# A mixed attention and spectral kernel: even row frequencies split once more, four of eight folds moved late, first loads in fixed order

## The chip, the cores and the metric

The kernel runs on one core of a Trainium2 chip. The metric is the device time of one execution in microseconds (us). Engines are named as the profile names them: PE is TensorE (PEld its weight loads), DVE is VectorE, ACT is ScalarE, POOL is GpSimd, SP is SyncE, which here only issues transfers.

## The reference, cut to what matters

```python
x = A_x                                   # (1, 2048, 640), fp32
g = sigmoid((x * gate_w).sum(-1, keepdims=True))
# a: attention with 32 heads of 20 over 8 positions s, s-2, ..., s-14
qkv = x @ wqkv
logits = einsum("bhsd,bhswd->bhsw", q, kg) * scale      # masked where s - 2w < 0
a = einsum("bhsw,bhswd->bhsd", softmax(logits), vg) reshaped @ wo
# b: a filter in the two-dimensional spectrum
X = rfft2(x) * (B_w_r + 1j * B_w_i)
b = irfft2(X, s=(2048, 640))
return g * a + (1 - g) * b
```

## The kernel before, in words

The 2048 positions are laid out as 128 partitions by 16 columns j (position 16p + j), called `NJ`. Even and odd j are treated apart, since attention steps by two.

**Projection** (`qkv`, line 703). Eight calls, one for each parity and each of four head groups. Each handles eight j; for one j fifteen multiplications (the operands split in a high and a low fp32r part, three products for each of five row chunks) sum 480 columns in one PSUM bank, taken in turn from `BP`, seven banks. ScalarE copies the bank to `ev`, and each second copy is stored to `qkv_d` in device memory.

**Attention** (`attend`, line 743). Sixteen units (parity, h) of four heads in the order `UNITS`. A unit loads keys, queries and values; for four pairs of rows jj it makes the products `pr` (on VectorE with the query in PSUM, or on GpSimd where `POOL_PR` says so), reduces them on VectorE to `L`, does the softmax, then makes `pv` on GpSimd and reduces it on VectorE to `o`, which goes to `o_d`. The last two units run pair by pair.

**Folds** (`fold`, line 824). The row transform of x over its 640 features uses symmetry: for each pair q of columns j, the row is folded into sums and differences of mirrored elements, twice, in place, in six instructions: 320 for odd frequencies, 320 for even ones, cosine and sine apart. Folds 0 to 5 are stored to `f_d` and reloaded by `load_f` (line 845); 6 and 7 stay. `cols` (line 849) then multiplies each by a table over partitions (twenty fp32 instructions `z` for one q) and ScalarE puts the result in `zg`, whose place is that of `xe`, the even inputs of the projection.

**Frequency groups** (`freq`, line 871). Sixteen groups g. `row` multiplies five chunks of `zc` by `bt`: three multiplications for `v`, three for `u`, of 321, 161 and 160 columns. Then column steps `xa` to `xd`, the filter `wp` (GpSimd and VectorE), and `g` back to `zg`. **Spatial** (`spatial`, line 996) goes back over features with `gt` (`oa`, `ob`) and over partitions (`ha`, `hb`); odd j keep theirs in `ho`, even j finish. **Even and odd projections** (`project_even`, `project_odd`, lines 1078 and 1094) load attention's result, transpose it (`oTp`), and multiply by `wo` (`woa`, `wob`, thirty multiplications for each j). Even ones are done as soon as the even units are; odd ones are last, and `ye` and `y` sum their spectral part on GpSimd.

**What sets the order.** Every operation is recorded by `Plan.record` first. `Plan.order` then gives each a cost (`Plan.cost`), runs a list scheduler backward and forward several times, disturbs the due times `AGAIN` times (`MOVE`, `SEED`) and keeps the best; `Plan.issue` emits the operations in that fixed order (line 639 is where they are issued, and so stands in all rows of the trace). Loads from inputs get an earliest time (`op.early`). Each engine's queue is in order; so is each issuing queue.

Of the kernel before, what the change touches and what calls it, by code (L numbers as in the profile page):

```python
# [31 lines left out]
def dft_tables():  # L32
# [7 lines left out]
    ke, ko = PERM[:161], PERM[161:]  # L40
    kb = PERM[2:161]
# [9 lines left out]
    def half(n, *ends):  # L51
# [3 lines left out]

    bt = np.zeros((640, 642))
    bt[0:161, 0:161] = np.cos(tau * np.outer(np.arange(161), ke) / D) * half(161, 0, 160)
    bt[161:321, 161:321] = np.cos(tau * np.outer(np.arange(160), ko) / D) * half(160, 0)
    bt[321:480, 323:482] = -np.sin(tau * np.outer(np.arange(1, 160), kb) / D)
    bt[480:640, 482:642] = -np.sin(tau * np.outer(np.arange(1, 161), ko) / D) * half(160, 159)  # L60
# [58 lines left out]
    d = np.arange(161)  # L119
# [5 lines left out]
    gt[0:161, 0:161] = np.cos(tau * np.outer(ke, d) / D) * ck(ke)  # L125
    gt[161:321, 161:322] = np.cos(tau * np.outer(ko, d) / D) * ck(ko) * (d < 160)
    gt[321:480, 322:483] = -np.sin(tau * np.outer(kb, d) / D) * ck(kb) * ((d > 0) & (d < 160))
    gt[480:640, 483:644] = -np.sin(tau * np.outer(ko, d) / D) * ck(ko) * (d > 0)
    gt = np.concatenate(
        [gt[0:128, 0:161], gt[128:256, 0:322], gt[256:384, 161:483], gt[384:512, 322:644], gt[512:640, 483:644]], 1  # L130
    )
    f = np.float32
    return {
        "t_fc": np.concatenate([fc, back[0].T, back[1].T], 1).astype(f),
# [7 lines left out]
class Op:  # L142
    __slots__ = ("i", "eng", "name", "call", "busy", "lat", "size", "preds", "succs", "chain", "tail", "start", "end", "early", "group", "of", "two")
# [12 lines left out]
class Plan:  # L156
# [65 lines left out]
    def record(self, eng, name, fn, a, k):  # L222
        op = Op()
        op.i, op.eng, op.name, op.chain, op.group = len(self.ops), eng, name, self.chain, self.group
        op.preds, op.succs, op.size, op.early, op.two = set(), [], 0, False, False
# [15 lines left out]
    def cost(self, op, out, ins, k):  # L241
        n = max(int(np.prod(v.shape[1:])) for v in [out] + ins[:1])
        if op.name == "dma_start":
            op.busy, op.lat = {"SP": 0.45, "ACT": 0.45, "POOL": 1.0}[op.eng], LAND
            op.size = int(np.prod(out.shape)) * 4
            op.early = not hasattr(ins[0].tensor, "tag")
        elif op.eng == "PE":
            n = int(np.prod(out.shape[1:]))
            if op.name == "transpose":
                op.busy = 0.109  # L250
            elif ins[-1].dtype == F32R:
                op.busy = n / 2400 + 0.018
            else:
                op.busy = 4 * n / 2400 + 0.006
# [23 lines left out]
    def order(self):  # L278
# [134 lines left out]
    def forward(self):  # L413
# [10 lines left out]
        while len(done) < len(ops):  # L424
# [47 lines left out]
TURNS, AGAIN, MOVE, SEED = 6, 100, 2.0, 2  # L472
# [7 lines left out]
FOLD = 14.0  # L480
# [25 lines left out]
class Mixer:  # L506
# [17 lines left out]
    def places(self, pp, dr, sb):  # L524
# [26 lines left out]
        self.er, self.xor = ring("e0", "e1"), ring("raw0", "raw1", "raw2", "raw3", "raw4", "kv4", "kv5", "ya")  # L551
# [8 lines left out]
        self.yr, self.yir = ring("raw3", "raw4", "e0", "ya"), n("f", 2)  # L560
# [10 lines left out]
    def work(self):  # L571
# [6 lines left out]
        st = [t[:, i] for t in (self.xr.next(f"st{i}", 2, 641) for i in range(7)) for i in range(2)]  # L578
        self.load_x(st, xe[:, 0], 0)
# [3 lines left out]
        self.xr.turn = 0  # L583
# [616 lines left out]
```

## Time and profile before

| | |
|---|---|
| median of 3 runs | 456.91 us (456.4 to 458.68) |
| the profiled execution | 457.05 us |
| its span, first to last instruction | 455.2 us |
| PE busy | 444.1 us, 98%, 2437 instructions |
| DVE busy | 408.0 us, 90%, 499 instructions |
| POOL busy | 344.2 us, 76%, 299 instructions |
| ACT busy | 211.0 us, 46%, 562 instructions |
| moved by DMA | 102.20 MB |
| granted TensorE clock | full in every slice |

Busy time is the time in which an engine had at least one instruction running. Starts that follow each other closer than one instruction lasts are overlap within the engine's pipeline, so a step is read from start to start where rows allow it.

### The profile page before, as it was taken

The page shows a single profiled execution, that of the slowest core. Times are in us where ns is not written, and L with a number is a line of the kernel's source. Part 1 is how long each engine was busy: PE and PEld are TensorE (multiplying, and loading weights), DVE is VectorE, ACT ScalarE, POOL GpSimd, SP SyncE. Part 2 cuts the span into 40 slices and gives each one's busy share as a digit, 9 for nine tenths or more (in the row PEclk, how much of TensorE's full clock was granted, in tenths as well). Part 3 has the DMA queues.
Part 4 walks back from the last instruction along what each step waited for, and adds up shares of the span by engine and source line. Part 5 has one row for each costly group of instructions (what it writes and reads, how often), then busy time and mean ns, then how long its engine had stood idle before and what let it go on. Part 6 is the DMA issues. An engine that isn't in the chain of part 4 may idle for free.

```text
span 455.2 us, 7081 instructions
## 1 busy us (share of the span) xinstructions
PE 444.1 (98%) x2437; PEld 390.1 (86%) x2437; DVE 408.0 (90%) x499; ACT 211.0 (46%) x562; POOL 344.2 (76%) x299
## 2 busy tenths in 40 slices
PE   8999999999999999999998999999999999999996
PEld 4888888888888888988987789878988999998996
DVE  4499999899999999999999999999999999799433
ACT  4734162424413223344367888786765563342120
POOL 1394056799999878998949894958597688888794
PEclk9999999999999999999999999999999999999999
DMA  8999998766636829989898666756653331255842
GB/s 303 411 398 295 380 355 286 238 192 224 199 95 216 267 67 268 374 261 324 241 362 291 199 213 193 265 178 200 204 160 120 88 98 57 80 189 182 274 147 87
DMA packets 70307, 102.20 MB, mean 224 GB/s; under 512 B 20464, under 2 KB 48240, under 8 KB 70272
## 3 DMA queue, kind: packets, MB, share of 16 engines
q1 hardware_dynamic: 38464, 66.20, 43.4%
q10 hardware_dynamic: 31760, 35.48, 24.1%
q8 instruction: 19, 0.31, 0.3%
q14 instruction: 16, 0.13, 0.1%
q0 software_dynamic: 48, 0.07, 0.0%
HBM read 68.90 MB, written 32.84 MB: 223 GB/s over the span
## 4 chain that ended last, share of the span: by engine, by line
DVE 44%; PE 25%; DMA 15%; issue 7%; POOL 4%; ACT 3%; ACTq 1%; SPq 0%; DVEq 0%; POOLq 0%
DMA qkvd<-ev 7%; PE woa L639 6%; PE wob L639 5%; PE g L639 2%; PE oa L639 2%; DVE xd L639 2%; PE ob L639 2%; PE u L639 2%; PE v L639 2%; DVE fx L639 1%; POOL pv0b L639 1%; DMA xt<-in_xT 1%; DMA od<-o1b 1%; DMA st<-in_w 1%; PE oTp L639 1%
## 5 line engine op out<-in xcount | busy, mean ns | idle before, releaser
L639 PE MATMUL qkv<-w,xo 128*128 128x480 f32 (+1 forms) x480 | 115.8, 388 | 0.0
L639 PE MATMUL qkv<-w,xe 128*128 128x480 f32 (+1 forms) x465 | 103.5, 382 | 0.0
L639 PEld LDWEIGHTS qkv<-w,xe 128*128 128x128 f32 x465 | 87.6, 188 | 14.6 <-issue 0.2
L639 PEld LDWEIGHTS qkv<-w,xo 128*128 128x128 f32 x480 | 89.1, 189 | 12.6
L639 PE MATMUL woa<-wo,oT 128*128 128x320 f32 x240 | 50.9, 319 | 0.0
L639 PE MATMUL wob<-wo,oT 128*128 128x320 f32 x240 | 50.8, 318 | 0.0
L639 ACT COPY ev<-qkv 128x480 f32<-128x480 f32 x64 | 35.3, 556 | 32.2 <-DMA qkvd<-ev 15.8
L639 PEld LDWEIGHTS wob<-wo,oT 128*128 128x128 f32 x240 | 39.0, 188 | 0.7 <-ACT ya L639 0.3
L639 PEld LDWEIGHTS woa<-wo,oT 128*128 128x128 f32 x240 | 38.9, 189 | 0.5
L639 POOL TENSOR_TENSOR w<-raw,w 128x480 fp32r<-128x480 f32 x15 | 19.5, 1328 | 26.2 <-ACT w L639 25.7
L639 POOL TENSOR_TENSOR P<-X,wp 128x642 f32<-128x642 f32 x16 | 24.9, 1558 | 17.3 <-ACT X L639 17.2
L639 ACT CAST oT<-oTp 128x384 fp32r<-128x384 f32 (+1 forms) x32 | 13.5, 427 | 29.8 <-PE oTp L639 17.6
L639 PEld LDWEIGHTS g<-mm,s 128*128 128x128 f32 x150 | 21.6, 190 | 6.3 <-issue 1.9
L639 POOL TENSOR_TENSOR xo<-xt,xo 128x640 fp32r<-128x640 f32 x8 | 14.6, 1857 | 16.4 <-ACT xo L639 16.4
L639 DVE TENSOR_TENSOR oT<-oTp,oT 128x384 fp32r<-128x384 f32 (+1 forms) x32 | 15.1, 485 | 12.1 <-ACT oT L639 11.9
L639 PE MATMUL g<-mm,s 128*128 128x128 f32 x150 | 24.2, 279 | 1.5 <-DVE s L639 0.7
L639 PE MATMUL oa<-gt,zg 128*128 128x161 f32 (+1 forms) x96 | 23.0, 344 | 0.0
L639 PE MATMUL v<-bt,zc 128*128 128x321 f32 (+2 forms) x96 | 22.4, 345 | 0.4 <-ACT zc L639 0.4
L639 PE MATMUL u<-bt,zc 128*128 128x321 f32 (+2 forms) x96 | 22.7, 344 | 0.0
L639 PE MATMUL ob<-gt,zg 128*128 128x161 f32 (+1 forms) x96 | 22.6, 344 | 0.0
L639 PEld LDWEIGHTS z<-fc,f 128*128 128x128 f32 x120 | 19.1, 191 | 1.5
L639 DVE TENSOR_TENSOR fx<-fx 128x642 f32<-128x642 f32 (+2 forms) x21 | 19.7, 975 | 0.3
(299 smaller groups left out, 1105.9 us busy)
## 6 DMA issues: line engine op xcount, KB each, us to landing
qkvd<-ev ACTq DMA_DIRECT2D x32, 480.0 KB, 4.7
wp<-in_ws SPq DMA_DIRECT2D x16, 642.0 KB, 4.5
fx<-in_x SPq DMA_DIRECT2D x8, 641.0 KB, 8.5
ot<-od SPq DMA_DIRECT2D x16, 320.0 KB, 3.2
fd<-fx ACTq DMA_DIRECT2D x6, 640.0 KB, 9.2
f<-fd SPq DMA_DIRECT2D x6, 640.0 KB, 5.9
raw<-in_wqkv SPq DMA_DIRECT2D x15, 240.0 KB, 5.5
xt<-in_xT SPq DMA_DIRECT2D x8, 320.0 KB, 6.4
```

The costliest lines, as they stand in the source:

```text
L639: p.dve.memset(w, 0.0)
```

## The change

- `PERM` puts odd frequencies first, then the even ones as 2, 6, 10, ... and as 4, 8, ..., 0, 320. A fold splits the even half a third time, so that of 321 cosine outputs 160 are odd, 80 and 81 are the two even kinds (likewise for sine). `row` then needs 321 + 81 + 160 columns, not 321 + 161 + 160, for `v` and for `u`.
- Odd j go back by a new table `g4` (in the place of `bt`) with 324 + 81 + 162 columns; `project_odd` gets seven instructions of sums, not five. Even j keep a table `gt` with the old split in the new order.
- `fold` now has 14 VectorE instructions, each with one operand in PSUM (banks 4 to 6), two ScalarE copies to put it there, and a ScalarE instruction of one column. All eight run on VectorE. Folds 0 and 1 are made early and kept, 2 and 3 (`STORED`) early and stored, 4 to 7 late, in the buffers that the `z` steps before them set free.
- `qkv` and `z` use four PSUM banks, 0 to 3.
- The first loads get a rank, which fixes their order: even inputs and first weights, rows for folds 0 and 1, then odd inputs.
- GpSimd makes the products of jj = 6 in all units; the sums of odd projections 13 and 15 go to VectorE; three steps of the gates go to ScalarE; the unit (1, 2) stands before (0, 4).
- The planner tries 250 disturbances, each near one point of time, and counts a small fp32 multiplication as at least 0.182 us.

```diff
-PERM = np.array([0, 320] + list(range(2, 320, 2)) + list(range(1, 320, 2)))
+PERM = np.array([*range(1, 320, 2), *range(2, 320, 4), *range(4, 320, 4), 0, 320])
+BQ, BF = (0, 1, 2, 3), (4, 5, 6)
...
+            if self.rank:
+                op.rank, self.rank = self.rank, self.rank - 1.0
...
-                op.busy = 4 * n / 2400 + 0.006
+                op.busy = max(4 * n / 2400 + 0.006, 0.182)
...
-            op.early = max(FOLD * (op.chain == "fold"), span - op.tail - AHEAD) if op.early else 0.0
+            op.early = max(FOLD * (op.chain == "fold"), span - op.tail - AHEAD) if op.early and not op.rank else 0.0
...
-            move *= rng.random(len(names)) < rng.choice([0.1, 0.5, 1.0])
-            for op, t in zip(ops, (best[1] + move[family]).tolist()):
+            move *= rng.random(len(names)) < rng.choice([0.02, 0.1, 0.5])
+            a = rng.uniform(0, span)
+            width = rng.choice([30.0, 100.0, 500.0])
+            near = np.abs(np.array([op.start for op in ops]) - a) < width
+            for op, t in zip(ops, (best[1] + move[family] * near).tolist()):
...
-                heappush(ready[e], (-op.tail, op.i, r, op))
+                heappush(ready[e], (-op.tail - op.rank, op.i, r, op))
...
-TURNS, AGAIN, MOVE, SEED = 6, 100, 2.0, 2
+TURNS, AGAIN, MOVE, SEED = 6, 250, 2.0, 2
...
+        p.rank = 1e6
         self.load_x(st, xe[:, 0], 0)
         self.load_w(st, 0)
         for j in range(2, NJ, 2):
             self.load_x(st, xe[:, j // 2], j)
         self.xr.turn = 0
+        self.fold(0)
+        self.fold(1)
+        rank, p.rank = p.rank, 0.0
         S.dma_start(self.fc, ins["t_fc"][:, 0:128])
         self.zero_rows()
         self.qkv(0, 0)
-        for q in range(8):
-            self.fold(q)
+        p.rank = rank
         for j in range(1, NJ, 2):
             self.load_x(None, self.xr.next(f"xo{j}", 2, 5, 128, dtype=F32R), j)
+        p.rank = 0.0
+        for q in STORED:
+            self.fold(q)
...
-        todo = [6, 7, 0, 1, 2, 3, 4, 5]
+        todo = list(range(8))
...
-                self.cols(todo.pop(0))
-                if len(todo) > 1:
-                    self.load_f(todo[1])
+                q = todo.pop(0)
+                self.cols(q)
+                if q + 2 in STORED:
+                    self.load_f(q + 2)
+                elif q < 6:
+                    self.fold(q + 2)
...
+        self.g4 = self.one("g4", 1134, tag="e0")
+        self.p.sp.dma_start(self.g4, ins["t_g4"])
...
-            b = self.ps(BP, f"qkv{u}_{jj}")
+            b = self.ps(BQ, f"qkv{u}_{jj}")
...
-        p.dve.tensor_scalar_add(self.g, self.g, 1.0)
+        p.act.add(self.g, self.g, 1.0)
         p.dve.reciprocal(self.g, self.g)
-        p.dve.tensor_scalar_sub(self.nng, self.g, 1.0)
-        p.dve.tensor_scalar(out=self.ng, in0=self.g, scalar1=-1.0, scalar2=1.0, op0=ALU.mult, op1=ALU.add)
+        p.act.add(self.nng, self.g, -1.0)
+        p.act.mul(self.ng, self.nng, -1.0)
...
-        e = self.er.next(f"fe{q}", 2, 321)
-        f, o = xt[:, :, 0:640], xt[:, :, 0:321]
-        rv = xt[:, :, 640:319:-1]
-        G.tensor_add(e, o, rv)
-        G.tensor_sub(o, o, rv)
-        G.tensor_sub(f[:, :, 321:480], o[:, :, 1:160], o[:, :, 319:160:-1])
-        G.tensor_add(f[:, :, 480:640], o[:, :, 1:161], o[:, :, 319:159:-1])
-        G.tensor_add(f[:, :, 0:161], e[:, :, 0:161], e[:, :, 320:159:-1])
-        G.tensor_sub(f[:, :, 161:321], e[:, :, 0:160], e[:, :, 320:160:-1])
+        e = self.er.next(f"fe{q}", 2, 161)
+        bl, eh, oh = (
+            self.ps(BF, f"f{n}{q}")[:, 0:322].rearrange("p (r d) -> p r d", r=2) for n in ("lo", "eh", "oh")
+        )
+        p.act.copy(eh, rv[:, :, 160:321])
+        p.act.copy(bl, rv[:, :, 0:161])
+        V.tensor_sub(oh, o[:, :, 160:321], eh)
+        V.tensor_add(eh, o[:, :, 160:321], eh)
+        V.tensor_add(e, o[:, :, 0:161], bl)
+        V.tensor_sub(o[:, :, 0:161], o[:, :, 0:161], bl)
+        V.tensor_add(f[:, :, 480:640], o[:, :, 1:161], oh[:, :, 159::-1])
+        ah, al = bl[:, :, 0:80], o[:, :, 0:80]
+        V.tensor_sub(ah, o[:, :, 80:160], oh[:, :, 80:0:-1])
+        V.tensor_sub(al[:, :, 1:80], o[:, :, 1:80], oh[:, :, 159:80:-1])
+        V.tensor_sub(f[:, :, 321:400], al[:, :, 1:80], ah[:, :, 79:0:-1])
+        V.tensor_add(f[:, :, 400:479], al[:, :, 1:80], ah[:, :, 79:0:-1])
+        p.act.mul(f[:, :, 479:480], ah[:, :, 0:1], 2.0)
+        ah, al = oh[:, :, 0:81], eh[:, :, 80:161]
+        V.tensor_sub(f[:, :, 0:160], e[:, :, 0:160], eh[:, :, 160:0:-1])
+        V.tensor_add(ah, e[:, :, 80:161], eh[:, :, 80::-1])
+        V.tensor_add(e[:, :, 0:81], e[:, :, 0:81], eh[:, :, 160:79:-1])
+        V.tensor_sub(f[:, :, 160:240], e[:, :, 0:80], ah[:, :, 80:0:-1])
+        V.tensor_add(f[:, :, 240:321], e[:, :, 0:81], ah[:, :, 80::-1])
...
-        row(v, 4, bt[:, 803:1124], True, False)
-        row(v[:, 0:161], 3, bt[:, 642:803], False, False)
-        row(v[:, 161:321], 5, bt[:, 1124:1284], False, True)
+        row(v, 4, bt[:, 643:964], True, False)
+        row(v[:, 240:321], 3, bt[:, 562:643], False, False)
+        row(v[:, 0:160], 5, bt[:, 964:1124], False, True)
...
+        if j % 2:
+            g4 = self.g4
+            mm(o1[:, 0:324], 1, g4[:, 162:486], True, False)
+            mm(o1[:, 0:81], 2, g4[:, 486:567], False, False)
+            mm(o1[:, 162:324], 0, g4[:, 0:162], False, True)
...
-ODD_POOL = tuple(range(1, 16, 2))
+ODD_POOL = (1, 3, 5, 7, 9, 11)
...
-POOL_PR = {u: (6,) for u in ((0, 3), (0, 4), (0, 5), (0, 7), (1, 0), (1, 1), (1, 3), (1, 4), (1, 5), (1, 7))}
+POOL_PR = {(p, h): (6,) for p in range(2) for h in range(8)}
...
-UNITS = ((0, 0), (0, 1), (1, 0), (1, 1), (0, 2), (0, 3), (0, 4), (0, 5), (0, 6), (0, 7), (1, 2), (1, 3), (1, 4), (1, 5), (1, 6), (1, 7))
-FOLDS = ("pr0", "pr1", "pv0", "pv1", "f0", "f1", "f0", "f1")
+UNITS = ((0, 0), (0, 1), (1, 0), (1, 1), (0, 2), (0, 3), (1, 2), (0, 4), (0, 5), (0, 6), (0, 7), (1, 3), (1, 4), (1, 5), (1, 6), (1, 7))
+STORED = {2: 'pv0', 3: 'pv1'}
```

## Rows read from the trace of the kernel before

**Rows 1.** Stages: stretch, length, busy us of each engine (instructions), clock, DMA share, GB/s.
```profile
11.00:160.00 149.00, 149.00 (x681) 128.08 (x680) 139.44 (x133) 54.90 (x146) 105.55 (x79) 1.00 0.80 272
160.00:236.00 76.00, 76.00 (x427) 68.00 (x426) 75.23 (x64) 29.80 (x81) 65.22 (x51) 1.00 0.84 271
236.00:342.00 106.00, 101.69 (x606) 86.93 (x604) 100.19 (x166) 81.22 (x227) 82.21 (x71) 1.00 0.67 215
342.00:412.00 70.00, 69.00 (x434) 62.92 (x435) 66.49 (x88) 33.76 (x88) 57.36 (x49) 1.00 0.33 106
412.00:455.20 43.20, 39.27 (x275) 38.66 (x273) 21.62 (x44) 5.78 (x14) 31.89 (x44) 1.00 0.52 174
```

**Rows 2.** Waits of PE from 225 to 420: total us, times, longest us.
```profile
PE oTp L639 <- DVE oT L639: 1.6, 4, 0.6
PE xa L639 <- DVE ab L639: 1.3, 1, 1.3
PE g L639 <- DVE s L639: 0.7, 1, 0.7
```

**Rows 3.** Instructions in order, near 405: start us, us, engine, what.
```profile
402.29 1.48 DVE L639 TENSOR_REDUCE o7b<-pv7b 128x160 f32<-128x1280 f32 x1
...
408.56 0.38 PE L639 MATMUL oTp<-ident,ot 128*128 128x128 f32 x2
```

**Rows 4.** Instructions of PE in order, at 250 and 349.
```profile
249.68 0.61 PE L639 MATMUL g<-mm,s 128*128 128x128 f32 x4
250.12 0.44 PE L639 MATMUL v<-bt,zc 128*128 128x160 f32 x2
...
349.00 0.44 PE L639 MATMUL oa<-gt,zg 128*128 128x161 f32 x2
349.27 0.44 PE L639 MATMUL ha<-os,fct 128*128 128x161 f32 x2
```

**Rows 5.** Fold tile `fx` alone, 14 to 100: PE, PEld, DVE, POOL busy.
```profile
14.00:100.00 86.00, 0.00 (x0) 0.00 (x0) 35.53 (x42) 7.09 (x6) 1.00 0.90 316
```

**Rows 6.** Instructions of DVE in order, at 333 and 396.
```profile
332.57 0.48 DVE L639 TENSOR_TENSOR p<-xc,wp 128x321 f32<-128x321 f32 x1
332.97 0.49 DVE L639 TENSOR_TENSOR xd<-xd,wp 128x321 f32<-128x321 f32 x1
...
396.15 0.39 DVE L639 SCALAR_TENSOR_TENSOR h<-ha,ng,h 128x161 f32<-128x161 f32 x1 [1.56 <-ACT os L639]
396.45 0.38 DVE L639 SCALAR_TENSOR_TENSOR h<-ha,nng,h 128x160 f32<-128x160 f32 x1
```

**Rows 7.** Chain that ended last, three pieces: start us, us, what.
```profile
41.28 3.10 DMA q0a<-qkvd
...
53.13 1.41 DVE pr0a L639
...
118.92 1.39 DVE pr1a L639
```

**Rows 8.** Groups by shape on POOL: busy us, mean ns, idle before.
```profile
L639 POOL TENSOR_TENSOR pr4a<-kt4a,q4a 128x1280 f32<-128x1280 f32 x1 | 3.0, 2997 | 0.0
```

**Rows 9.** Instructions of DVE in order, the gates.
```profile
152.06 0.99 DVE L639 TENSOR_SCALAR g<-g 128x16 f32<-128x16 f32 x1
153.09 0.25 DVE L639 RECIPROCAL g<-g 128x16 f32<-128x16 f32 x1
153.37 3.80 DVE L639 TENSOR_SCALAR ng<-g 128x16 f32<-128x16 f32 x1
...
157.25 1.49 DVE L639 TENSOR_REDUCE L2a<-pr2a 128x64 f32<-128x1280 f32 x1
```

**Rows 10.** Waits of ACT over the whole span, those for a store of `ev`.
```profile
ACT ev L639 <- DMA qkvd<-ev: 15.8, 5, 7.1
```

**Rows 11.** Instructions on tile `z`, first kept folds: duration ns, first and last start.
```profile
L639 PE MATMUL z<-fc,fx x40: 270/275/275, 172.0 to 183.2; 128*128 128x128 f32 x40
```

**Rows 12.** Instructions of PE in order, the last `z`.
```profile
233.72 2.39 PE L639 MATMUL z<-fc,f 128*128 128x128 f32 x20
```

**Rows 13.** The page's DMA issues: KB each, median us to landing.
```profile
fx<-in_x SPq DMA_DIRECT2D x8, 641.0 KB, 8.5
f<-fd SPq DMA_DIRECT2D x6, 640.0 KB, 5.9
```

More of the change, by code (lines that the diff above doesn't have):

```diff
@@ L54, in half, with cos, sin @@
         return w[:, None]
+    def cos(n, k, first=0):
+        return np.cos(tau * np.outer(np.arange(first, first + n), k) / D)
+    def sin(n, k):
+        return -np.sin(tau * np.outer(np.arange(1, n + 1), k) / D)
     bt = np.zeros((640, 642))
[L57 to L60, printed above, removed]
+    bt[0:160, 0:160] = cos(160, ko) * half(160, 0)
+    bt[160:240, 160:240] = cos(80, k2) * half(80, 0)
+    bt[240:321, 240:321] = cos(81, k0) * half(81, 0, 80)
+    bt[321:400, 561:640] = sin(79, k0[:79])
+    bt[400:480, 481:561] = sin(80, k2) * half(80, 79)
+    bt[480:640, 321:481] = sin(160, ko) * half(160, 159)
     bt = np.concatenate(
-        [bt[0:128, 0:161], bt[128:256, 0:321], bt[256:384, 161:482], bt[384:512, 321:642], bt[512:640, 482:642]], 1
+        [bt[0:128, 0:160], bt[128:256, 0:321], bt[256:384, 240:321], bt[256:384, 561:642], bt[384:512, 321:642], bt[512:640, 321:481]], 1
     )
-    j, k2 = np.arange(16), np.arange(16)
+    j, kk = np.arange(16), np.arange(16)
     md = np.zeros((16, 16, 2, 4, 2, 16, 4))
@@ L142 @@
 class Op:
-    __slots__ = ("i", "eng", "name", "call", "busy", "lat", "size", "preds", "succs", "chain", "tail", "start", "end", "early", "group", "of", "two")
+    __slots__ = ("i", "eng", "name", "call", "busy", "lat", "size", "preds", "succs", "chain", "tail", "start", "end", "early", "group", "of", "two", "rank")
 class Engine:
@@ L224, in record @@
         op.i, op.eng, op.name, op.chain, op.group = len(self.ops), eng, name, self.chain, self.group
-        op.preds, op.succs, op.size, op.early, op.two = set(), [], 0, False, False
+        op.preds, op.succs, op.size, op.early, op.two, op.rank = set(), [], 0, False, False, 0.0
         line = sys._getframe(2).f_lineno
@@ L825, in fold @@
         p = self.p
-        G = p.dve if q in FOLD_DVE else p.pool
-        xt = self.one(f"fx{q}", 2, 641, tag=FOLDS[q])
-        p.chain = "fold"
+        V = p.dve
+        if q in STORED:
+            xt = self.one(f"fx{q}", 2, 641, tag=STORED[q])
+        else:
+            xt = self.fr.next(f"fx{q}", 2, 641)
+        p.chain = "fold" if q in STORED else ""
         p.sp.dma_start(xt, self.ins["x"][:, 2 * q : 2 * q + 2, :])
         p.chain = ""
-        e = self.er.next(f"fe{q}", 2, 321)
@@ L901, in freq @@
         u = self.ps(BU, f"u{g}")[:, 0:321]
-        row(u, 1, bt[:, 161:482], True, False)
-        row(u[:, 0:161], 0, bt[:, 0:161], False, False)
-        row(u[:, 161:321], 2, bt[:, 482:642], False, True)
+        row(u, 1, bt[:, 160:481], True, False)
+        row(u[:, 240:321], 2, bt[:, 481:562], False, False)
+        row(u[:, 0:160], 0, bt[:, 0:160], False, True)
         ab = self.abr.next(f"ab{g}", 2, 321)
@@ L1003, in mm @@
             T.matmul(o, zg[:, t, j], r, start=start, stop=stop, skip_group_check=True)
-        mm(o1[:, 0:322], 1, gt[:, 161:483], True, False)
-        mm(o1[:, 0:161], 0, gt[:, 0:161], False, False)
-        mm(o1[:, 161:322], 2, gt[:, 483:644], False, True)
-        mm(o2[:, 0:322], 3, gt[:, 805:1127], True, False)
-        mm(o2[:, 0:161], 2, gt[:, 644:805], False, False)
-        mm(o2[:, 161:322], 4, gt[:, 1127:1288], False, True)
-        os = self.osr.next(f"os{j}", 644)
+        if j % 2:
[3 more added lines that the diff above has]
+            mm(o1[:, 162:324], 0, g4[:, 0:162], False, True)
+            mm(o2[:, 0:324], 3, g4[:, 648:972], True, False)
+            mm(o2[:, 81:162], 2, g4[:, 567:648], False, False)
+            mm(o2[:, 162:324], 4, g4[:, 972:1134], False, True)
+        else:
+            mm(o1[:, 0:322], 1, gt[:, 160:482], True, False)
+            mm(o1[:, 0:161], 2, gt[:, 482:643], False, False)
+            mm(o1[:, 161:321], 0, gt[:, 0:160], False, True)
+            mm(o2[:, 0:322], 3, gt[:, 804:1126], True, False)
+            mm(o2[:, 0:161], 2, gt[:, 643:804], False, False)
+            mm(o2[:, 162:322], 4, gt[:, 1126:1286], False, True)
+        w = 162 if j % 2 else 161
+        os = self.osr.next(f"os{j}", 4 * w)
         oq = os.rearrange("p (b a d) -> p a b d", b=2, a=2)
-        A.copy(oq[:, 0], o1[:, 0:322].rearrange("p (b d) -> p b d", b=2))
-        A.copy(oq[:, 1], o2[:, 0:322].rearrange("p (b d) -> p b d", b=2))
+        A.copy(oq[:, 0], o1[:, 0 : 2 * w].rearrange("p (b d) -> p b d", b=2))
+        A.copy(oq[:, 1], o2[:, 0 : 2 * w].rearrange("p (b d) -> p b d", b=2))
         yield
@@ L1029, in spatial @@
             if j % 4 == 1:
[L1030 removed]
+                self.hpair = self.hor.next(f"ho{j}", 2, 2, 2, 162)
             h = self.hpair[:, j % 4 // 2]
[L1032 to L1033 removed]
+            A.mul(h[:, 0].rearrange("p b d -> p (b d)"), h1[:, 0:324], ng)
+            A.mul(h[:, 1].rearrange("p b d -> p (b d)"), h2[:, 0:324], ng)
             self.ho = getattr(self, "ho", {})
```

69 lines of the change are left out of this document (42 added, 27 removed).

## The prediction

> **What bounds the kernel now.** I read the stages first (busy time of each engine in five stretches), because a share over the whole span hides which engine ends what. The reader is to see in [rows 1] that TensorE is busy for all of 11 to 236 us, idle for 4.3 us of the 106 between 236 and 342, for 1.0 us of the next 70, and for 3.9 us of the last 43; nearly all of that last part is the drain of the final rows. VectorE is nearly as full: 139 of 149 us, 75.2 of 76, 100 of 106, 66.5 of 70, and only behind 412 half idle. GpSimd has 11 to 44 us left per stretch. So two engines are full at once, and TensorE is the one whose work reaches the end: it leaves 5.3 us on the table between 236 and 412 and nothing before. Second, the waits of TensorE in that part: the largest are for VectorE, 1.6 + 1.3 + 0.7 us [rows 2]. Third, the end: the first reduction of the last two attention units for position pair 0 starts at 402.29 and the first transpose of an odd projection at 408.56 [rows 3]; behind it lie eight odd projections, all TensorE. So the end moves if TensorE gets through its work earlier *and* the last attention units get done earlier too; either alone gives little.
>
> All sums are made against the profiled execution, 457.05 us, whose span is 455.2 (1.85 us around it); the median of the runs is 456.91, so the two scales are the same to 0.1 us.
>
> **Part 1, fewer columns on TensorE.** In each of 16 frequency groups, `v` and `u` each lose one multiplication of 161 columns and get one of 81; in each of 8 odd spatial steps `o1` and `o2` do the same. That is 32 + 16 = 48 multiplications. An fp32 multiplication is two instructions in the trace; one of 161 columns takes 349.27 - 349.00 = 0.27 us, start to start [rows 4]. One of 81 is not in the trace. Low end: in proportion to columns, 0.27 x 81/161 = 0.137. High end: the nearest row below 161, the 128-column one, two of them in 250.12 - 249.68 = 0.44, so 0.22 each [rows 4]; fewer columns have no reason to cost more. I take the middle, 0.18, as neither end has a row nearer to it. Saved: 48 x 0.09 = 4.3 us, bounds 48 x 0.05 = 2.4 and 48 x 0.133 = 6.4. The odd steps also widen 322 to 324 and 161 to 162 columns, 7 columns a step or 0.1 us over all eight, within the rounding.
>
> What speaks for the high end is a rule. The 128-column row shows 0.22 us, which its columns alone explain (128/161 x 0.27 = 0.215). The Trainium skill, "TensorE: Matmul & The Clock Gate", section "LDWEIGHTS (loading the stationary operand)", says that loading the stationary operand takes a time that only its own columns set, an estimate of 107 ns for 128 of them and so 0.21 us for the two loads of an fp32 multiplication, however few columns then stream; if loads cannot hide behind so short a step, the saving would be about 2.6 us, not 4.3. The row cannot tell the two, as both give 0.21 to 0.22 at 128 columns.
>
> **Part 2, the folds on VectorE.** Seven of eight folds run there now, the eighth on GpSimd: 42 instructions in 35.5 us, and 6 in 7.1 us [rows 5]. After, all eight run on VectorE with 14 instructions each, one operand in PSUM (put there by two ScalarE copies): six of 320 or 322 elements, eight of 158 to 162. The nearest rows with an operand in PSUM: 321 elements, 332.97 - 332.57 = 0.40 from start to start; 161 elements, 396.45 - 396.15 = 0.30 [rows 6], while by elements alone the small ones would be 0.24. One fold is 6 x 0.40 + 8 x 0.24 to 0.30 = 4.3 to 4.8, eight are 35 to 38. So the eighth fold is nearly free: 0 to +3 us, I take +1.5. GpSimd loses 7.1.
>
> **Part 3, other VectorE work.** GpSimd takes the products of rows 6 and 7 in all 16 attention units, not in ten: VectorE loses 6 x 1.4 = 8.4 us [rows 7], GpSimd gains 6 x 3.0 = 18 [rows 8]. The three scalar steps of the gates leave VectorE for ScalarE: from 152.06 to 157.25, less one product of 1.4 and 0.3 for the reciprocal that stays, 3.5 us [rows 9]. Ahead of the end of attention VectorE thus does 1.5 - 8.4 - 3.5 = -10 us (bounds -12 to -9), GpSimd 18 - 7.1 = +11. GpSimd has 43 + 11 + 24 + 13 = 91 us of idle time in these four stretches [rows 1], but only 11 of 76 between 160 and 236. ScalarE gets 8 x 2 copies and a few small ones, under 10 us, and it has 46 us free in the stretch with the late folds. The sums of two odd projections move from GpSimd to VectorE, behind 412, where VectorE is half idle: nothing; if that cover were gone, some 6 us (14 instructions at 0.40).
>
> **Part 4, where the freed VectorE time goes.** TensorE can use it only where it waits for VectorE: 3.6 us [rows 2]. I take half, 1.8, bounds 0 and the whole 5.3 us of idle time between 236 and 412.
>
> **Part 5, what is moved.** *First loads in fixed order, and only four folds early.* TensorE has no idle time from 11 to 236, so nothing is gained there; VectorE now folds until 53.1, though the first query of attention landed at 41.28 + 3.10 = 44.4 [rows 7]. Four folds fewer there let attention start up to 9 us sooner, and the same four come back between 160 and 236: a swap, net 0 for VectorE. Four stores and four reloads of 640 KB go. *Folds 4 to 7 late.* Each now sits between the load of its rows (median 8.5 us [rows 13]) and its `z` multiplications, in a buffer that must be free first; it is priced under the rivals, 0 here as the sum there leaves slack. The loads stand on SyncE's queue, behind stores of attention results that wait for VectorE; the folds stand in VectorE's queue ahead of attention. *Four banks, not seven, for `qkv` and `z`.* ScalarE must empty a bank within three groups of 15 multiplications, about 9.8 us at 0.219 each (149 us for 681 instructions [rows 1]); the longest time a copy out of them waited was 7.1 us, for a store [rows 10]. So 0, and up to 2 us if waits add up. *The new table `g4`* takes the place of `bt`, so its load waits for the last row transform, and the odd spatial steps wait for it; before them lie the column steps of the last groups, so 0 (bounds 0 to 3). *Unit (1,2) ahead of (0,4)* makes the even projections, TensorE's filler, later by up to one unit; VectorE's gain of up to 10 us covers most of it: 0 (0 to 3). *More tries of the planner* choose among orders: unknown sign, no row prices it; I give it 1 us either way in the range.
>
> **The sum.** 457.05 - 4.3 - 1.8 + 0 = 450.95, say 451.0. With all bounds good 457.05 - 6.4 - 5.3 = 445.4; with the poor ends of parts 1 and 4, and 2 us of the moved steps, 457.05 - 2.4 + 2 = 456.7.
>
> **Rivals.** *A, attention's end holds the gate.* If VectorE's -10 us are eaten by waits (folds for copies and loads, reductions for a GpSimd that has 18 us more to do), pair 0 is still reduced at 402 and the first odd transpose still comes at 408.56 [rows 3], and TensorE's 4.3 us become idle time in front of it: 455 to 457. Against it: 10 us is more than twice what is needed. For it: GpSimd was busy 65 of 76 us between 160 and 236. *B, the columns save nothing,* an 81-column step costing as the 161 one: 457.05 - 1.8 = 455.3. Against it: the 128 row is shorter than the 161 row. *C, slower: the late folds starve TensorE at the change from `qkv` to the row transforms.* The first `z` of all starts at 172.0 [rows 11] and the last group ends at 233.72 + 2.39 = 236.1 [rows 12]. With f for one late fold, one of the two buffers goes: `z` 2.4 us (twenty instructions [rows 12]), reload 5.9 [rows 13], `z` 2.4, load 8.5, f, `z` 2.4, load 8.5, f, `z` 2.4. That ends at 172 + 32.5 + 2f, and no row transform can start sooner. Against 236 it decides from f = 16 us on; at 4.5 us of VectorE and 1 of ScalarE, and VectorE giving half its time to two folds at once, f is about 10. At f = 20 TensorE idles 8 us: 457.05 - 4.3 + 8 = 460.8. For it: VectorE has 0.8 us free in those 76. *D, more heals than I took*: the column steps near the low end and most of the idle time gone, 446.
>
> **Chances.** The forecast 0.56 (own range 448 to 454.5), D 0.10, A 0.13, B 0.05, C 0.16. A measurement of this kernel tells 0.5%, 2.3 us, from no change. Faster: forecast and D, 0.66; same: A and B, 0.18; slower: C, 0.16. Range: 446 to 460 leaves out less than half of D below and about half of C above, near 2 in 10 with what is not thought of.
>
> **What the profile after would show.** TensorE's busy time lower by 2.4 to 6.4 us, all of it in the `u`, `v`, `oa`, `ob` groups, and an 81-column pair with a step between 0.137 and 0.22. Attention starting near 44 instead of 53. VectorE lower by about 9 us ahead of 412, GpSimd's products there up by 18. The last `z` still no later than the last `qkv`, with less than 1 us of TensorE idle in front of the first `v`. The forecast is wrong if TensorE shows idle time between 220 and 245 (C), if the first odd transpose comes no earlier than 405 (A), or if new waits for GpSimd stand in VectorE's list in the first 160 us.

## The result, and the profile after

The changed kernel takes 458.45 us (median of 20 runs, 456.0 to 464.7), the kernel before 456.73 beside it. One of its 20 runs was in a slower state and is left out of the ratio and of every comparison below; the median of the other 19 is 458.16. The ratio is 1.0045, 95% interval 1.0031 to 1.0059: 1.4 us slower by the medians and 2.1 by the ratio, where 6 us faster was forecast. It lies inside the range, but the direction was wrong.

The stages of the changed kernel, columns as in [rows 1]. The profiled execution took 460.58 us, span 458.8, so it shows about 2 us more loss than the median does.

```profile
11.00:160.00 149.00, 144.73 (x661) 124.08 (x660) 132.40 (x154) 58.93 (x164) 113.82 (x85) 1.00 0.74 244
160.00:236.00 76.00, 75.04 (x411) 66.70 (x410) 71.25 (x100) 28.88 (x78) 59.06 (x45) 1.00 0.77 237
236.00:342.00 106.00, 100.98 (x606) 85.25 (x605) 102.16 (x164) 81.16 (x226) 82.46 (x69) 1.00 0.71 230
342.00:412.00 70.00, 69.26 (x443) 63.14 (x442) 65.23 (x88) 34.70 (x90) 61.69 (x52) 1.00 0.38 115
412.00:458.80 46.80, 42.67 (x299) 41.86 (x297) 29.44 (x64) 7.89 (x20) 31.90 (x44) 1.00 0.49 155
```

Read the first number behind the length, TensorE. In the first 149 us, where it had no idle time at all [rows 1], it now stands for 4.27 us, and from 160 to 236 for 0.96. Between 236 and 342 it stands for 5.02 us (4.31 before). VectorE, two columns on, has 371.0 us of work ahead of 412, not 381.4. Some of these 10 us are only steps that slipped behind 412, since this kernel runs later: in e1 below, which ends with the kernel before, it is 373.6, so 7.7 us less. No gain came of them. VectorE's idle time is now in front: 16.6 us of the first 149 (9.6 before) and 4.75 of the next 76 (0.8).

Whole-span busy times on the page of the changed kernel:

```profile
PE 442.3 (96%) x2437; PEld 387.0 (84%) x2437; DVE 405.3 (88%) x574; ACT 217.6 (47%) x583; POOL 350.9 (76%) x301
```

TensorE is busy 1.8 us less, not 4.3. The new idle time in the first 160 us has one cause by the list of waits of TensorE (total us, times, longest), here 11 to 160:

```profile
PE qkv L683 <- ACT ev L683: 2.7, 1, 2.7
PE qkv L683 <- ACT z L683: 1.6, 1, 1.6
```

`ev` and `z` are the two copies with which ScalarE empties a bank of a projection group. The place of the longer wait, instructions in order, first of TensorE and then of ScalarE (start, duration, engine, what, and in brackets the idle time before it and what ended it):

```profile
61.18 8.89 PE L683 MATMUL qkv<-w,xe 128*128 128x480 f32 x40
72.73 3.52 PE L683 MATMUL qkv<-w,xe 128*128 128x480 f32 x15 [2.66 <-ACT ev L683]
```

```profile
68.44 0.21 ACT L683 COPY L0b<-low 1x16 f32<-1x16 f32 x1 [1.68 <-DVE L0b L683]
...
72.02 0.21 ACT L683 COPY L0b<-low 1x16 f32<-1x16 f32 x1 [2.53 <-DVE L0b L683]
72.13 0.54 ACT L683 COPY ev<-qkv 128x480 f32<-128x480 f32 x1
```

The copy at 72.13 waited for no data of its own. It stood in ScalarE's queue behind small mask copies of attention that waited for VectorE, and with four banks TensorE had no other bank to go to (e1 below tests this). Near 33 it was a store and then other copies, of ScalarE again:

```profile
30.59 0.56 ACT L683 COPY ev<-qkv 128x480 f32<-128x480 f32 x1 [2.42 <-DMA qkvd<-ev]
...
32.41 1.36 ACT L683 CAST xo<-xt 128x640 fp32r<-128x640 f32 x2
33.66 0.45 ACT L683 COPY flo<-fx 128x322 f32<-128x322 f32 x1
34.02 0.57 ACT L683 COPY ev<-qkv 128x480 f32<-128x480 f32 x1
```

The waits of TensorE from 225 to 420, to be held against [rows 2]:

```profile
PE xc L683 <- DVE s L683: 1.1, 1, 1.1
PE oTp L683 <- DVE oT L683: 0.9, 1, 0.9
PE v L683 <- ACT vs L683: 0.8, 1, 0.8
PE xa L683 <- DVE ab L683: 0.7, 2, 0.4
PE u L683 <- DVE ab L683: 0.7, 2, 0.4
...
PE xa L683 <- DVE p L683: 0.4, 1, 0.4
```

Those for VectorE were 3.6 us and are 1.1 + 0.9 + 0.7 + 0.7 + 0.4 = 3.8. Some healed and others came, most of them in the chain of column steps (`ab`, `xa`, `xc`, `s`), which less work on VectorE did not shorten.

The end: the reductions of attention's last unit, of the kernel before and of the changed one (shortest, median and longest ns, first and last start), then the first transpose of an odd projection, against [rows 3], and the first attention product on VectorE, against [rows 7]:

```profile
L639 DVE TENSOR_REDUCE o7b<-pv7b x4: 1474/1476/1486, 393.1 to 419.7; 128x160 f32<-128x1280 f32 x4
```

```profile
L683 DVE TENSOR_REDUCE o7b<-pv7b x4: 1475/1476/1486, 402.0 to 425.1; 128x160 f32<-128x1280 f32 x4
```

```profile
412.73 0.38 PE L683 MATMUL oTp<-ident,ot 128*128 128x128 f32 x2
```

```profile
52.01 2.88 DVE L683 TENSOR_TENSOR pr0a<-kt0a,qbank 128x1280 f32<-128x1280 f32 x2 [6.09 <-DMA kt0a<-qkvd]
```

The row at 402.29 in [rows 3] is the second of these four reductions, not the first, which comes at 393.1. So attention's last unit did not get earlier: its first reduction comes 9 us later and its last 5 us later. The first transpose of the odd projections comes 4.2 us later, behind TensorE's own work: TensorE's list shows no wait from 395 up to it. Attention did not start at 44 us: its first product waited for the load of its keys until 52.0. The prediction had read when the query lands, 44.4; the keys land at 49 already in the trace of the kernel before.

### The profile page after: what moved, and what is told of

Read it like the earlier page. It is cut to its first block, busy times and chain, and to the rows that moved or that the text cites. A ratio compares the mean times of both kernels' runs of the same rounds, so it can differ in the third digit from the quotient of the medians.

```text
span 458.8 us, 7197 instructions
## 1 busy us (share of the span) xinstructions
PE 442.3 (96%) x2437; PEld 387.0 (84%) x2437; DVE 405.3 (88%) x574; ACT 217.6 (47%) x583; POOL 350.9 (76%) x301
## 5 line engine op out<-in xcount | busy, mean ns | idle before, releaser
L683 PE MATMUL qkv<-w,xo 128*128 128x480 f32 (+1 forms) x480 | 113.3, 386 | 2.6 <-ACT z L683 1.6
L683 PE MATMUL woa<-wo,oT 128*128 128x320 f32 x240 | 52.2, 318 | 0.6 <-ACT oT L683 0.6
L683 POOL TENSOR_TENSOR xo<-xt,xo 128x640 fp32r<-128x640 f32 x8 | 12.8, 1618 | 22.7 <-DMA xt<-in_xT 19.9
L683 PE MATMUL g<-mm,s 128*128 128x128 f32 x150 | 22.5, 277 | 0.6 <-ACT zg L683 0.6
L683 PE MATMUL v<-bt,zc 128*128 128x321 f32 (+2 forms) x96 | 21.0, 338 | 1.2 <-ACT vs L683 0.8
L683 PE MATMUL u<-bt,zc 128*128 128x321 f32 (+2 forms) x96 | 20.5, 336 | 0.7 <-DVE ab L683 0.7
L683 PEld LDWEIGHTS v<-bt,zc 128*128 128x128 f32 x96 | 14.8, 190 | 4.6 <-ACT vs L683 1.3
L683 PEld LDWEIGHTS u<-bt,zc 128*128 128x128 f32 x96 | 15.0, 191 | 4.3 <-PE xa L683 0.9
L683 PEld LDWEIGHTS z<-fc,fx 128*128 128x128 f32 x120 | 17.1, 191 | 1.0
L683 PE MATMUL z<-fc,fx 128*128 128x128 f32 x120 | 17.1, 275 | 0.0
```

The lines of the kernel that those rows point to most:

```text
L683: p.dve.memset(w, 0.0)
```

## The experiments

Where it says that the order is kept, the planner is left out and the instructions are issued in the list that it had found for the kernel named, so that nothing moves but the part that is edited. Four questions were asked.

**Are four banks the cause?** e1 gives the projection calls that run while no fold uses the other banks all seven again, in the changed kernel's order:

```diff
+FREE = ((0, 1), (1, 1), (0, 2), (0, 3))
...
-            b = self.ps(BQ, f"qkv{u}_{jj}")
+            b = self.ps(BP if (par, hg) in FREE else BQ, f"qkv{u}_{jj}")
```

> The changed kernel with its order of instructions held fixed, and seven PSUM banks for the projection in the four calls between which no fold stands (parity 0 head group 1 to parity 0 head group 3); four elsewhere. Theory 1 (four banks are too few: TensorE waits for ScalarE to empty one): the 2.7 us of idle time near 70 us go, the 1.6 us near 33 us stay; about 456 us, 2 to 3 us below the changed kernel. Rival (the time lost early is not what sets the end; attention on VectorE and GpSimd holds the gate): the idle time near 70 goes but comes back behind 236, time as the changed kernel, 458.5.

Measured: 456.60 us, ratio to the kernel before 0.9992 (0.9978 to 1.0007). The first four stages of e1, and TensorE's waits in the first two:

```profile
11.00:160.00 149.00, 147.73 (x676) 126.98 (x675) 133.56 (x154) 60.42 (x166) 115.73 (x86) 1.00 0.76 249
160.00:236.00 76.00, 75.41 (x420) 67.16 (x419) 73.09 (x104) 30.14 (x80) 58.88 (x46) 1.00 0.78 239
236.00:342.00 106.00, 100.81 (x604) 85.03 (x603) 101.59 (x164) 81.39 (x227) 82.81 (x68) 1.00 0.70 224
342.00:412.00 70.00, 69.18 (x442) 62.94 (x442) 65.40 (x88) 34.52 (x89) 63.21 (x53) 1.00 0.39 118
```

```profile
PE qkv L789 <- ACT z L789: 1.3, 1, 1.3
PE qkv L789 <- ACT ev L789: 0.6, 1, 0.6
```

The wait near 72 is gone and the one near 33, in one of the first two calls, which still have four banks, stays. By the medians the banks cost 458.16 - 456.60 = 1.6 us, by the ratios 0.53% or 2.4. Part of that is the clock granted to TensorE: four runs of the changed kernel have a mean of 0.996 and take 459.8 to 462.1 us, while the median of the other fifteen is 458.10; in e1 none is below 0.999. e9 is the other side, that part of the change alone in the kernel before and its order:

```diff
-            b = self.ps(BP, f"qkv{u}_{jj}")
+            b = self.ps(BQ, f"qkv{u}_{jj}")
...
-            z = self.ps(BP, f"z{q}_{t0}")
+            z = self.ps(BQ, f"z{q}_{t0}")
```

> The kernel before with one part of the change alone: the qkv groups and z take turns in four banks of PSUM instead of seven; its order of instructions is kept (three of 3576 stand one place later). Theory (four banks are too few because ScalarE's delays add up): in the kernel before the copies already run up to 8.7 and 9.0 us behind the groups, with four banks holding out 9.8, so its own order comes close to the limit but seldom over it: 0 to +2 us, ratio 1.000 to 1.004, with waits of a qkv group for a copy of ev or z in the trace between 11 and 240 us. Rival (four banks cost what they cost in the changed kernel, 1.9 us, whatever the order): ratio 1.004. Rival (seven banks gained in the changed kernel for another reason than waits): no new wait and 1.000.

Measured: 459.23 us beside 456.99, ratio 1.0054 (1.0037 to 1.0070). TensorE's wait of e9 for these copies, 11 to 240:

```profile
PE qkv L743 <- ACT ev L743: 1.3, 3, 0.5
```

It is new, before the groups at 200.8, 209.9 and 220.7; the kernel before had no idle time of TensorE up to 236 [rows 1]. The ratio lies above my upper bound of 1.004, which its interval still holds, and the rival that they cost the same whatever the order fits. The profiled execution of e9 (457.99 us, the fastest of its six) shows these 1.3 us of waits where the medians lose 2.2; where the rest goes is not shown. That four banks cost some 2 us is thus shown from both sides, in one order each.

**What are fewer columns worth?** e2 fills the two new tables with zero columns, so that the 48 multiplications of 81 columns have 161 again; e7 is the same on e1. Both keep the order.

```diff
-        row(v[:, 240:321], 3, bt[:, 562:643], False, False)
+        row(v[:, 160:321], 3, bt[:, 642:803], False, False)
...
-            mm(o1[:, 0:81], 2, g4[:, 486:567], False, False)
+            mm(o1[:, 0:161], 2, g4[:, 486:647], False, False)
```

> The changed kernel, order held fixed, with each of the 48 multiplications of 81 columns made 161 columns wide again (the added columns of the table are zero). If an 81-column multiplication saves 0.09 us each, as forecast, TensorE is busy 4.3 us longer and the time is about 462.5; if it saves 0.05 (a step of one row transform is 1.04 us against 1.09 in the trace of before), 2.4 us and 461; if it saves nothing that reaches the end, 458.5.

Measured: 459.03 us, ratio 1.0044 (1.0024 to 1.0065).

> e1_banks7 with the 48 multiplications made 161 columns wide again, order held fixed: the cost of the columns without the early waits that blur it in e2_wide. At 0.05 us each 2.4 us more than e1_banks7, 459.0; at 0.09, 4.3 us more, 461; if the columns are hidden by other waits, 0 to 1 us, 457.

Measured: 457.22 us, ratio 1.0003 (0.9978 to 1.0027). By the medians, undoing the columns costs 0.9 us in e2 against the changed kernel and 0.6 in e7 against e1; by the ratios it costs nothing and 0.5. All of that lies inside the intervals. The groups of TensorE by shape (busy us, mean ns of one) in e1, with 81 columns, and in e7, those of `v` (`u` is the same to 1 ns or 0.1 us):

```profile
L789 PE MATMUL v<-bt,zc 128*128 128x160 f32 x32 | 7.5, 316 | 0.0
...
L789 PE MATMUL v<-bt,zc 128*128 128x81 f32 x32 | 5.5, 254 | 0.0
```

```profile
L789 PE MATMUL v<-bt,zc 128*128 128x161 f32 x32 | 7.0, 300 | 0.0
L789 PE MATMUL v<-bt,zc 128*128 128x160 f32 x32 | 7.0, 299 | 0.0
```

The short multiplication saves 1.5 us in a group of 32 instructions, and the one of 160 columns behind it takes 0.5 of that back, though nothing in it changed. A whole row of three in order, from the start of `u` to that of `xa`, is 256.41 - 255.37 = 1.04 us in e1 and 256.99 - 255.91 = 1.08 in e7:

```profile
255.37 1.20 PE L789 MATMUL u<-bt,zc 128*128 128x321 f32 x6
256.41 1.25 PE L789 MATMUL xa<-ab,tbfirst 128*128 128x321 f32 x4
```

```profile
255.91 1.25 PE L789 MATMUL u<-bt,zc 128*128 128x321 f32 x6
256.99 1.25 PE L789 MATMUL xa<-ab,tbfirst 128*128 128x321 f32 x4
```

That pair gives 0.04 us a row. The rows of `v` that run without a break, seven in either trace, take 1.036 us in e1 and 1.086 in e7 (medians, start to start), so 0.05. That is 2 to 2.4 us in 48 rows; TensorE's busy time of the two differs by 443.7 - 442.2 = 1.5.

**Is VectorE's time worth anything?** e12 puts the gates' steps back on VectorE, and e13 runs the sums of the late folds over one row of two and leaves the other row unfolded. Both stand on e1 and keep its order.

```diff
-        p.act.add(self.g, self.g, 1.0)
+        p.dve.tensor_scalar_add(self.g, self.g, 1.0)
...
-        p.act.add(self.nng, self.g, -1.0)
-        p.act.mul(self.ng, self.nng, -1.0)
+        p.dve.tensor_scalar_sub(self.nng, self.g, 1.0)
+        p.dve.tensor_scalar(out=self.ng, in0=self.g, scalar1=-1.0, scalar2=1.0, op0=ALU.mult, op1=ALU.add)
```

> The changed kernel with seven banks for four qkv calls (e1) and the three scalar steps of the gates back on VectorE, order kept: +3.5 us of VectorE's work near 150 us. Theory (VectorE's freed time ahead of the late folds became idle time and waits): 0 to +1 us against e1's 456.6. Rival (VectorE's time reaches the end at half its size or more): +1.8 to +3.5 us, 458.4 to 460.

Measured: 456.40 us, ratio 0.9988 (0.9971 to 1.0005), beside e1's 456.60. This tells little: the steps stand at 65 to 73 us in this order, not near 150, and VectorE's busy time rose by 0.8 us (405.1 to 405.9), not by 3.5.

```diff
+        def brief(op):
+            return op if q < 4 else lambda out, a, b: op(out[:, 0:1], a[:, 0:1], b[:, 0:1])
+        add, sub = brief(V.tensor_add), brief(V.tensor_sub)
...
-        V.tensor_sub(oh, o[:, :, 160:321], eh)
+        sub(oh, o[:, :, 160:321], eh)
```

> e1 with the 14 VectorE instructions of each of the late folds 4 to 7 run over one of the two rows, so half the elements; the other row is left unfolded, so this leaves out a quarter of the folding. Order kept. By the rows of the changed kernel (0.49 us at 322 elements, 0.32 at 160) a fold gets some 1.5 us shorter, four of them 6 us, in the stretch from 200 to 237 us. Theory (the late folds stand on the chain: they eat the lead of attention and hold up z): TensorE's waits behind 236 us get shorter, 2 to 5 us less than e1's 456.6, so 452 to 455. Rival (the end isn't VectorE's in this order): within 0.7 us of e1.

Measured: 456.17 us, ratio 0.9982 (0.9970 to 0.9994). The page of e13, and its second and third stage:

```profile
PE 441.6 (97%) x2437; PEld 386.3 (85%) x2437; DVE 398.8 (88%) x574; ACT 218.1 (48%) x583; POOL 350.5 (77%) x301
```

```profile
160.00:236.00 76.00, 76.00 (x423) 67.88 (x422) 70.04 (x107) 30.59 (x81) 59.20 (x47) 1.00 0.78 240
236.00:342.00 106.00, 101.58 (x612) 85.84 (x611) 99.38 (x162) 82.09 (x228) 82.53 (x68) 1.00 0.70 226
```

6.3 us less on VectorE (405.1 in e1) and an end 0.4 us earlier. My theory that the late folds hold up what follows them fell; the rival holds. TensorE waits 0.6 us less from 160 to 236 and 0.8 less to 342 than in e1, and little of that reaches the end.

e3 goes the other way, by a change of two parts: five banks for `qkv` and `z` (seven in the four calls of e1), and to make room one operand of the folds moves from PSUM to SBUF. Order kept.

```diff
-BQ, BF = (0, 1, 2, 3), (4, 5, 6)
+BQ, BF = (0, 1, 2, 3, 4), (5, 6)
...
+        self.flr = ring("flo")
...
-        bl, eh, oh = (
-            self.ps(BF, f"f{n}{q}")[:, 0:322].rearrange("p (r d) -> p r d", r=2) for n in ("lo", "eh", "oh")
-        )
+        bl = self.flr.next(f"flo{q}", 2, 161)
+        eh, oh = (self.ps(BF, f"f{n}{q}")[:, 0:322].rearrange("p (r d) -> p r d", r=2) for n in ("eh", "oh"))
```

> The changed kernel, order held fixed; one of the fold's three temporaries goes to SBUF, so that the projection and the column steps have five banks, and seven in the four calls between the folds. Theory 1: both early waits go, 4.3 us; about 454 to 454.5, a little below before. Rival (the gate is elsewhere): 458. The sums of the fold with both operands in SBUF may wait for GpSimd: 0 to 2 us of VectorE, later than 200 us.

Measured: 463.04 us, ratio 1.0129 (1.0106 to 1.0152), with VectorE at 414.1 us, 8.8 more than in the changed kernel. TensorE's waits from 11 to 300, three of the longest:

```profile
PE z L790 <- issue: 2.1, 1, 2.1
...
PE xa L790 <- DVE ab L790: 1.4, 2, 1.1
PE z L790 <- DVE fx L790: 1.3, 1, 1.3
```

For the first line the profile shows no cause. The last is a late fold that comes too late for its `z`, which rival C of the prediction spoke of. So VectorE's time looks one-sided in this order: 6 us less gain 0.4, while 9 more cost 6 against e1. But e3 also changes the banks of the folds, of `z` and of the other `qkv` calls, so these 6 us need not be VectorE's alone.

**How much is the order itself?** e4 and e8 are the changed kernel and the kernel before with another seed of the planner, planned anew; nothing else differs.

```diff
-TURNS, AGAIN, MOVE, SEED = 6, 250, 2.0, 2
+TURNS, AGAIN, MOVE, SEED = 6, 250, 2.0, 3
```

> The changed kernel with another seed of the planner, nothing else. If the loss is the four banks (theory 1), any order meets waits of TensorE for ScalarE ahead of 160 us, 2 to 5 us in total, and the time is 458 to 462; if the loss is only this order's bad luck, the early waits are gone and the time is 454 or less.

Measured: 462.95 us, ratio 1.0125 (1.0098 to 1.0153).

> The kernel before with another seed of its planner, nothing else: what the luck of one order is worth. If the order of before was an ordinary draw, 455 to 459; if before was a lucky draw, 460 or more, and the change is then better than the direct comparison says.

Measured: 460.68 us, ratio 1.0066 (1.0033 to 1.0099). Its largest wait, at the change to the row transforms:

```profile
PE v L639 <- ACT zc L639: 4.6, 1, 4.6
```

A draw moves either kernel by 4 to 5 us, more than the change does. Not all of that is waits. In the profiled executions of e4, e5, e6, e8, e10 and e11, all newly planned, the clock granted to TensorE fell to 1.2 GHz for 3.4 to 6.8 us, during one of its waits or just after one. It did so in no other run's profiled execution before the last 3 us. The stretches of e8 and e6 that hold it (the clock is the third number from the end):

```profile
236.00:260.00 24.00, 19.29 (x92) 15.35 (x92) 19.03 (x28) 18.27 (x50) 16.84 (x15) 0.86 0.85 291
```

```profile
11.00:60.00 49.00, 45.32 (x194) 38.27 (x193) 35.89 (x93) 23.15 (x60) 16.41 (x11) 0.93 0.90 319
```

The one run of e8 with a mean clock of 1.000 took 458.10 us, the four with 0.991 took 460.3 to 462.1. That is why the next four, which place the folds elsewhere and are all planned anew, settle less than they were meant to. e5 makes all eight folds early; e6 has besides seven banks in six of the `qkv` calls and for `z`; e10 (another seed) and e11 make two and one more fold early and have the banks of e1.

```diff
-STORED = {2: 'pv0', 3: 'pv1'}
+STORED = {2: 'pv0', 3: 'pv1', 4: 'pr0', 5: 'pr1', 6: 'pv0', 7: 'pv1'}
```

> The changed kernel with its late folds undone: folds 2 to 7 all early and stored, as before the change (0 and 1 kept); the planner orders anew. Theory 2 (the four late folds take about 18 us of VectorE between 160 and 236, where TensorE's column steps and attention both wait for it; early they lie where VectorE idles): VectorE's idle time in 11 to 60 us goes from 15 back to about 8, attention's eleventh unit ends near 285 instead of 300, the first even projection comes earlier, time 453 to 455. Rival (four banks alone are the loss): the early waits of TensorE stay at 2 to 4 us and the time stays at 457 to 459.

> As e5_early_folds, and seven banks for the projection and the column steps in all calls behind the folds; the planner orders anew. If theories 1 and 2 both hold and add: 451 to 453, below both kernels. If only theory 2 holds: as e5_early_folds. If only theory 1 holds: 456.5, as e1_banks7.

> The changed kernel with folds 4 and 5 early too (stored and loaded back), only 6 and 7 late, seven banks for four of the qkv calls, planned anew with another seed. Theory (late folds take attention's lead; too many early ones starve the first groups): between all late and all early, so little idle time of TensorE on either side: 454 to 458, ratio 0.995 to 1.003. Rival (the planner's draw decides, not the place of the folds): anything from 455 to 463.

> The changed kernel with fold 4 early too and 5 to 7 late, seven banks for four of the qkv calls, planned anew. Theory: near e10, 455 to 459, with more waits of TensorE after 236 us than e10 and fewer before 60. Rival (the planner's draw): anything from 455 to 463.

Measured: e5 461.02 (ratio 1.0082, 1.0055 to 1.0109), e6 458.08 (1.0022, 1.0002 to 1.0041), e10 461.34 (1.0100, 1.0080 to 1.0119), e11 461.03 (1.0091, 1.0076 to 1.0105). The waits of e5, 11 to 160:

```profile
PE qkv L683 <- ACT ev L683: 3.1, 1, 3.1
PE qkv L683 <- ACT w L683: 3.1, 1, 3.1
PE qkv L683 <- ACT z L683: 2.6, 2, 1.5
```

With early folds and four banks the same two copies hold TensorE again, and casts of weights (`w`) besides; e6 with its banks is 3 us better, which agrees with the first question, though two draws can differ by as much. That a place between all early and all late is best did not come true: e10 and e11 are slower than e1 and e6 at either side. Whether the place or the draw decided, these runs cannot tell. No version that does the whole work beat the kernel before by more than the interval of its ratio. e6 may hold more than its time shows: none of its twelve runs has a mean clock above 0.996. In its profile some 5.7 us of TensorE's work ran at 1.2 GHz, so by my estimate from that (half of 5.7 us less) it would take some 455 us at full clock; no run shows it.

## Why the prediction was wrong, point by point

**What bounds the kernel.** The reading that two engines are full at once was wrong in what it was taken to mean. VectorE is 90% busy, but 7.7 us less in e1 brought no gain that can be seen, and 6 us less again in e13 brought 0.4. In these orders TensorE's work and waits carry to the end. The end was misread besides. The prediction took the row at 402.29 for the first reduction of pair 0, which comes at 393.1, and the transpose at 408.56 for one that waits for it. In the trace of the kernel before the loads of that pair's results start at 397.8 and land by 402.0, so this transpose too came behind TensorE's own work.

**Part 1, columns: right mechanism, term mis-sized.** 0.04 to 0.05 us a row was measured, not 0.09, so 2 to 2.4 us on TensorE where 4.3 were forecast, and 0 to 0.9 at the end where the sum passed on all of it. This is the largest miss of the sum, 3.4 us or more. The mistake was to price the multiplication alone: in the kernel it stands between two others, and the one behind it grew from 299 to 316 ns. The rule that was weighed there, from the Trainium skill, "TensorE: Matmul & The Clock Gate", section "LDWEIGHTS (loading the stationary operand)", gave 2.6 by its estimate; the trace, at 2 to 2.4, agrees with it rather than with my middle value. The rival that they save nothing (B) is nearer to what the end shows, though not to TensorE's 2.

**Part 2, folds: somewhat too low.** The instructions on tile `fx` take 17.66 us on VectorE early and 17.43 late, 35.1 in all:

```profile
14.00:100.00 86.00, 0.00 (x0) 0.00 (x0) 17.66 (x48) 4.17 (x12) 1.00 0.80 268
200.00:240.00 40.00, 9.69 (x75) 9.86 (x76) 17.43 (x48) 4.01 (x12) 1.00 0.81 238
```

These are 96 of the 112 instructions. The other 16, two in each fold, name only `fe`, `feh` and `foh`; with them VectorE is busy 39.5 us with folds, where 35 to 38 were forecast and the old folds took 35.5 [rows 5]. So the eighth fold costs 4.0 us, not 0 to 3.

**Part 3, VectorE's 10 us: too high.** 7.7 us less were measured (e1 ahead of 412), below the bound of 9, and the folds' 4.0 instead of 1.5 make most of the gap. The gates were priced at 3.5 us from the span of their rows [rows 9]; at their new place e12 shows 0.8 us, and what they cost at the old one was not run. GpSimd got 6.7 us more, not 11.

**Part 4, healed waits: failed.** 1.8 us forecast, none came: 3.6 us of waits for VectorE before, 3.8 after. They were read as a queue for a busy engine. The names in the list say that they are links of a chain in which TensorE and VectorE take turns, which a less busy VectorE does not shorten; that reading is argued, and e13's 0.8 us less idle time between 236 and 342 is all that a run shows for it.

**Part 5, four banks at 0: failed, and this is what turned the sign (without it, in e1, the ratio is 0.9992).** The tolerance of 9.8 us was held against the longest single wait of a copy, 7.1 us [rows 10]. What counts is how far ScalarE is behind in all when it comes to a bank: store waits, casts of the odd inputs, fold copies and mask copies that wait for VectorE stand in its one queue. The rows at 30 to 34 and 68 to 72 us show that; e1 and e9 price it at 1.6 to 2.5 us. The text did name "up to 2 us if waits add up" as the bound; the value taken was the wrong end of it.

**Part 5, the rest.** Attention at 44 us: wrong, as the load of the first keys landed only at 52. So it was no swap: the folds' early time became idle time of VectorE, and the late folds came on top. Late folds at 0: right at this size (e13), and of rival C's mechanism, a `z` that waits for a late fold, e3 shows 1.3 us. The planner's order at 1 us either way: too small, a draw moves 4 (e4, e8), of which the clock is a part.

**The sum again,** by what the runs show: -0.9 to 0 for columns, +1.6 to 2.4 for banks, 0 for healed waits. That is +0.7 to +2.4, and +1.4 to 2.1 was measured. What the other moves and the change of order bring between them is thus within a microsecond or so, but it is a remainder of numbers with intervals of 0.7 us or more: parts that cancel in it were not told apart. Where the saved 2 us of TensorE went shows in part in the stages of e1 against [rows 1]: idle ahead of 236 for 1.86 us against 0, between 236 and 342 for 5.19 against 4.31.

**The rivals.** A put the end at 455 to 457 with VectorE's 10 us eaten by waits and attention's end as the gate. The first half holds: in e1, with 7.7 us less work on VectorE, the reductions of the last unit still run from 398.3 to 421.3, later than before (393.1 to 419.7). The second does not: the first odd transpose comes behind TensorE's own work, at 408.97 in e1 as at 408.56 before. C's sign, idle time of TensorE between 220 and 245, showed only in small: 1.4 us before 245, one wait of 0.96 for ScalarE and one of 0.42. D is out.

## What to carry to other kernels

Before a ring of buffers is cut, add up all that stands in the queue of the engine that empties it, waits for other engines included, over the worst stretch, and hold that against the ring, not its longest single wait. Work taken from an engine at 90% need not pay at all; take some away by a cheap experiment with the order kept before you price it. Where a planner draws the order, a part of this size can be measured only with the order kept, and the forecast's range needs the spread between draws, here 4 us. Look at the granted clock of every run before you call one order better than another.

## What was not expected of the hardware

A multiplication of TensorE got slower because the one ahead of it got shorter: 160 columns, 299 ns behind one of 161 and 316 behind one of 81. By the starts of the single instructions in uninterrupted rows of `v` (medians), the two short ones of e1 are followed after 0.07 and 0.11 us and the next one, of 160 columns, after 0.18; in e7 each of these steps is 0.14.

Taking one operand of a VectorE sum from PSUM keeps it clear of GpSimd. In the changed kernel the late sums `fe<-fx,flo` of 322 elements, with `flo` in PSUM, take 477 to 485 ns; in e3, with it in SBUF, 485 to 1267 (lowest, median and highest duration on the tile):

```profile
L683 DVE TENSOR_TENSOR fe<-fx,flo x4: 477/481/485, 204.6 to 232.0; 128x322 f32<-128x322 f32 x4
```

```profile
L790 DVE TENSOR_TENSOR fe<-fx,flo x4: 485/944/1267, 203.1 to 232.9; 128x322 f32<-128x322 f32 x4
```

What lies beside it shows in e3, instructions of both engines in order:

```profile
203.65 3.21 POOL L790 TENSOR_TENSOR pr3a<-kt3a,q3a 128x1280 f32<-128x1280 f32 x1
204.12 3.09 DVE L790 TENSOR_TENSOR fx<-fx,flo 128x322 f32<-128x322 f32 x1
```

The sum with both operands in SBUF is over 0.35 us after GpSimd's product ends at 206.86, not 0.5 us after its own start. The Trainium skill, "SBUF — State Buffer", section "SBUF: two separate sides", says that the two engines share a pair of ports which one instruction holds to its end, also where VectorE reads two operands from SBUF; the two rows agree. VectorE is busy 39.5 us with the 112 fold instructions in e1 and 50.0 in e3, so the operand in PSUM explains the 9 us that it is busy longer there.
